# Token-order expert units in groups of four: one 128-row pass each, and four quarter-array passes side by side

## Chip, cores and metric

The kernel runs on 1 core of one Trainium2 chip. The metric is device time in microseconds (us): 950.32 us is the median of 3 runs of the kernel before (950.28 to 957.16). Engines are named as in the profile: PE is TensorE (PEld its weight loads), DVE is VectorE, ACT is ScalarE, POOL is GpSimd, SP is SyncE, which here only issues DMAs.

## What is computed

Four batches of 10048 tokens go through agent attention and then through a two-level mixture of experts. Cut to what matters:

```python
# B, N, C = 4, 10048, 128; 49 agents; 4 groups x 4 experts; F = 1024
a2k = softmax(scale * agents @ k.T)      # 49 x N per batch
agent_v = a2k @ v                        # 49 x 128
q2a = softmax(scale * q @ agents.T)      # N x 49
x = q2a @ agent_v                        # N x 128, rank 49
g = argmax(x @ w_group); e = argmax(x @ w_expert[g])    # one expert of 16 per token
h = relu(x @ w1[g, e])                   # 1024 wide
out = p(g) * p(e) * (h @ w2[g, e])       # p: softmax weights of the choices
```

## The kernel before

**Small rank.** A token's `x` has rank 49, so the kernel never forms it. It keeps the 49 exponentials of `q2a` per token (the tile `ef`), and multiplies `agent_v` (scaled, in the tile `at`) into an expert's `w1` once. An expert's first product is then a product over 49 rows, its second one over the 1024 columns.

**Two halves of a number.** All these products run in fp16 with each operand split into a high part and a low part (the rounded value and what is left of it). A tile `et` holds 512 tokens as columns; its rows 0 to 48 are the high parts, its rows 49 to 97 the low parts of the exponentials. A tile `wbuf` holds an expert's factors: 1024 columns of high parts, 1024 of low parts (both repeated for the two row blocks), then the two halves of `w2`.

**Units.** A unit is 128 of the 1024 columns for a tile of 512 tokens. It has a first product into a PSUM bank `ph`; an eviction (ACT: relu to fp16, tile `hh`; DVE: what is left of it, tile `hl`; `evicted`, line 1197); and a second product, 12 passes of 128 columns into the bank `po` (`second`). A tile of 512 tokens has 8 units and ends with `oo`, a DVE multiplication of `po` by the tokens' weights, and the DMA of the result (`out_rows`).

**Stages.** (1) A front of some 77 us for the first batch (batch 1): keys, values, agents, the first queries. (2) The token-order stage: the batches 1, 2, 3 in turn, each as 20 tiles of tokens in their own order, all with the expert that most of the batch's tokens choose: 60 tiles, 480 units (the last tile of each batch has 384 tokens). (3) The sorted stage: the tokens of batch 0, which were brought into the order of their experts by indirect DMAs, in 19 tiles of 512 and 3 of 256.

**First product, token order.** `first` (line 1204) makes two passes of 98 rows by 512 columns into one of three banks `ph`: the high factors, then the low ones. Up to 8 units lie between a first product and its second (`LAG`).

**First product, sorted.** `first_group` (line 1178) takes four units at once. Each has one pass of 128 rows: 98 rows as above with the high factors, and in the rows 98 to 127 the low factors of the first 30 agents against a copy of the high exponentials. The remaining 19 agents' low factors are four passes of 19 rows, which sit in the four quarters (32 rows each) of the array, one unit per quarter, and write four different banks. For these, a tile `rest` holds four copies of 19 rows of `et`, made by four DMAs on SP's queue (`turn`, line 1176). The banks are three of `ph` and those of the pool `at` in turn.

**Side work.** Beside the units of one batch, the next batches are prepared: scores of keys and queries (`at<-agh,xh` and its like), softmax over agents, routing, the turning of exponentials into `et` (`turned`), all as Python generators. `advance` (line 1375) is called once per unit; it lets lanes of `QUEUE` step while two budgets last (`RATE`: DVE and ACT nanoseconds per unit), the lane that is furthest behind its share (`QUEUE`, `TOTALS`) first. A generator that yields a number is left alone for so many units (`HOP` is 2), so that what it waits for is done by then. The tile framework then orders each engine's instructions; each engine runs its own list in order and waits on semaphores.

**Banks.** PSUM has eight banks: three for `ph`, two for `po`, three for `at` (the side work, and in the sorted stage half of the units).

## Time and profile before

| what | value |
|---|---|
| median of 3 runs | 950.32 us |
| the profiled execution's own time | 955.84 us |
| its span, first to last instruction | 954.1 us |
| mean granted TensorE clock | 0.970 |
| first `ph` of an expert unit, first `rest` pass | 76.8 us, 768.5 us |
| PE, DVE, ACT, POOL busy | 92%, 78%, 65%, 45% of the span |

How to read it: the two marks in the fifth row bound the stages. From 76.8 to 768.5 us lie the 480 token-order units with all side work, from there to 942.5 us (the last `po`) the sorted units with almost none, and some 12 us of closing follow. Busy time is a union of instructions; a PE matmul is shown from its start to its modelled end, some 160 ns after the next one has started, so a pass is timed from its start to the start of the next.

### The profile page before, as it was taken

To read this page: it belongs to the slowest core of one execution; us is meant where nothing else is said; L and a number is where in the kernel's file an instruction comes from. 1 tells how busy PE (TensorE), PEld (TensorE's weight loads), DVE (VectorE), ACT (ScalarE), POOL (GpSimd) and SP (SyncE) were. 2 spreads that over 40 slices of the span, in tenths; PEclk is the share of its full clock that TensorE was granted. 3 is DMA by queue.
4 is the path that set the end of the run, shared out by engine and by line. 5 is a ranking of instruction groups with operands and counts; after the bars stand their busy time and mean duration, and the time that the engine had idled before them with its cause. 6 is when DMAs were issued, how large, how long until landed. Compare 5 with 4: busy or idle time off the path is not lost.

```text
span 954.1 us, 31174 instructions
## 1 busy us (share of the span) xinstructions
PE 875.2 (92%) x12947; PEld 699.0 (73%) x12948; DVE 740.6 (78%) x1619; ACT 619.5 (65%) x1071; POOL 431.6 (45%) x573
## 2 busy tenths in 40 slices
PE   3868998999998989999999999999999999999985
PEld 2765876877776777777778777787777887777864
DVE  5646699889689797769988988989987666667753
ACT  4546777866877767668778677776556555555541
POOL 3164535533743235454355432465555414444434
PEclk9777999999999999999999999999999999999998
DMA  9637534535426444444435231222646445555560
GB/s 314 193 122 241 177 123 120 173 100 161 134 72 196 136 126 134 147 133 130 116 93 155 80 102 49 93 90 90 203 153 202 140 149 197 200 194 203 196 215 29
DMA packets 110461, 140.26 MB, mean 147 GB/s; under 512 B 8374, under 2 KB 90369, under 8 KB 107495
## 3 DMA queue, kind: packets, MB, share of 16 engines
q1 hardware_dynamic: 105159, 127.88, 42.3%
q0 software_dynamic: 5152, 10.30, 3.3%
q8 instruction: 103, 1.69, 0.7%
q14 instruction: 47, 0.39, 0.1%
HBM read 96.83 MB, written 39.99 MB: 143 GB/s over the span
## 4 chain that ended last, share of the span: by engine, by line
PE 54%; DVE 24%; issue 8%; ACT 5%; POOL 5%; DMA 3%; SPq 1%; POOLq 0%; ACTq 0%; DVEq 0%
PE po L135 28%; PE ph L135 15%; PE at L135 11%; DVE hl L135 8%; POOL xl L272 3%; DVE vl L135 3%; DVE S L135 2%; ACT hh L135 2%; DVE oh L135 1%; DMA out<-oo,er 1%; DVE oo L135 1%; DVE rx L135 1%; DVE mq L135 1%; POOL xs L272 1%; DVE ef L135 1%
## 5 line engine op out<-in xcount | busy, mean ns | idle before, releaser
L135 PEld LDWEIGHTS <-hh 128*128 128x128 f16 x5104 | 410.6, 98 | 122.4 <-issue 12.7
L135 PE MATMUL po<-wbuf,hh 128*128 128x128 f16 x5104 | 489.7, 220 | 0.9 <-ACT hh L135 0.8
L135 DVE SCALAR_TENSOR_TENSOR hl<-ph,hh 128x512 f16<-128x512 f32 (+1 forms) x562 | 377.2, 677 | 140.2 <-ACT hh L135 138.1
L135 PE MATMUL po<-wbuf,hl 128*128 128x128 f16 x2552 | 457.7, 220 | 0.0
L135 ACT ACTIVATE hh<-ph 128x512 f16<-128x512 f32 (+1 forms) x562 | 328.4, 592 | 190.3 <-PE ph L135 106.3
L135 PE MATMUL ph<-et,wbuf 98*128 98x512 f16 (+3 forms) x1048 | 319.1, 380 | 23.9 <-DVE hl L135 19.8
L272 POOL TENSOR_TENSOR xl<-xf,xh 128x256 f16<-128x256 f32 x280 | 187.8, 705 | 165.6 <-ACT xh L135 144.0
L135 PEld LDWEIGHTS <-hl 128*128 128x128 f16 x2552 | 249.4, 98 | 0.3 <-issue 0.3
L135 PEld LDWEIGHTS <-wbuf 98*128 98x128 f16 (+2 forms) x1412 | 99.5, 99 | 73.2 <-issue 45.3
L1253 POOL DMA_INDIRECT out<-oo,er x82 | 80.5, 981 | 111.9 <-ACT hh L135 60.7
L998 POOL DMA_INDIRECT sorted_rows<-rows,slot x79 | 78.5, 994 | 68.2 <-ACT hh L135 48.9
L135 ACT ACTIVATE xh<-xf 128x1280 f16<-128x1280 f32 (+2 forms) x59 | 73.5, 1251 | 26.3 <-PE at L135 9.7
L713 POOL TENSOR_TENSOR rows<-ef,rows 128x245 f16<-128x245 f32 (+1 forms) x62 | 41.1, 684 | 74.7 <-ACT rows L135 74.7
L479 POOL TENSOR_TENSOR sl<-S,sh 128x245 f16<-128x245 f32 (+2 forms) x51 | 35.1, 711 | 82.1 <-ACT sh L135 75.9
L135 PEld LDWEIGHTS <-xh 128*128 128x128 f16 (+1 forms) x1164 | 55.1, 99 | 3.8 <-issue 2.3
L135 PE MATMUL at<-agh,xl 128*128 128x49 f16 x523 | 52.2, 185 | 5.6 <-POOL xl L272 5.5
L135 DVE SCALAR_TENSOR_TENSOR hl<-at,hh 128x512 f16<-128x512 f32 x82 | 55.8, 681 | 0.0
L135 PEld LDWEIGHTS <-xl 128*128 128x128 f16 (+1 forms) x582 | 48.5, 98 | 7.5 <-POOL xl L272 7.0
L135 ACT ACTIVATE et<-at 98x512 f16<-98x512 f16 (+1 forms) x80 | 47.3, 593 | 10.4 <-PE at L135 9.9
L135 PE MATMUL at<-agh,xh 128*128 128x49 f16 x523 | 51.9, 186 | 0.6 <-ACT xh L135 0.6
L135 PE MATMUL at<-agl,xh 128*128 128x49 f16 x523 | 51.5, 185 | 0.0
L135 DVE SCALAR_TENSOR_TENSOR vl<-vf,vh 128x640 f16<-128x640 f32 (+2 forms) x51 | 44.8, 890 | 8.5 <-ACT vh L135 6.7
(268 smaller groups left out, 1053.4 us busy)
## 6 DMA issues: line engine op xcount, KB each, us to landing
wbuf<-wdr SPq DMA_DIRECT2D x22, 1024.0 KB
vf<-v SPq DMA_DIRECT2D x28, 640.0 KB
xf<-qT SPq DMA_DIRECT2D x28, 640.0 KB
xf<-kT SPq DMA_DIRECT2D x23, 640.0 KB
out<-oo SPq DMA_DIRECT2D x57, 256.0 KB
erow<-rows SPq DMA_DIRECT2D x12, 490.0 KB
er<-sorted_rows SPq DMA_DIRECT2D x19, 256.0 KB
wbuf<-kT SPq DMA_DIRECT2D x5, 640.0 KB
```

Of the source, the lines that this page charges most:

```text
L135: return f(*a, **k)
L272: pool.tensor_sub(out=xl[:, a:z], in0=xf[:, a:z], in1=xh[:, a:z])
L479: pool.tensor_sub(out=sl[0:m, y][:, z], in0=x[:, z], in1=sh[0:m, y][:, z])
L713: pool.tensor_sub(out=x0[:, a:z, NA:2 * NA], in0=ef[:, a:z], in1=x0[:, a:z, 0:NA])
L998: ins = pool.indirect_dma_start(out=sorted_rows[:, :], out_offset=bass.IndirectOffsetOnAxis(ap=at, axis=0), in_=x, in_offset=None, bounds_ ...
L1253: ins = pool.indirect_dma_start(out=out, out_offset=bass.IndirectOffsetOnAxis(ap=to, axis=0), in_=y, in_offset=None, bounds_check=B * N - ...
```

## The change

It does this:

- `first` goes. Token-order tiles use `first_group` too, for four units at a time: four passes of 128 rows, then the four quarter passes of 19 rows. The units of a group are no longer neighbours: group g has units g, g+2, g+4, g+6 of the 8, so that a quarter of the array always meets the same quarter of the columns; the low factors are stored once (`W2 = F + F // 4` columns ahead of `w2` where there were `2 * F`). The product of two low parts is left out, as in the sorted stage. The very first tile keeps two 98-row passes per unit (`"low" in x`).
- Rows 98 to 127 of `et` are now filled for all batches: `query_split` copies 30 high exponentials more per token (ACT), the transposes turn 128 columns.
- Every token-order tile gets its four `rest` DMAs, a tile ahead (`rest_ahead`).
- `expert_split` makes the mixed factors with one DVE operation more per half (`scalar_tensor_tensor` with the constant `head`), and four SBUF-to-SBUF DMAs for a token-order expert.
- PSUM: four banks for `ph`, one for `po` (two before), three for `at`.
- Pending second products: 4 to 8 units as the groups go, `LAG` is gone. Within a tile's first group side work follows each unit's second product; in its second group the four second products run first, then four `advance` calls in one place.
- The budgets become 700 and 900 with twice that as the most saved up; `HOP` now stands for 2 to 4 units, up to a fixed place in the next group; yields that need not wait so long are 1 or 2.

Cut to its core:

```diff
-RWS = [P // 2 + 2 if b == SORTED else NA for b in range(B)]
+RWS = [P // 2 + (2 if b == SORTED else 0) for b in range(B)]
-RATE = np.array([900.0, 1100.0])
+RATE = np.array([700.0, 900.0])
-HOP = 2
+HOP = 9
-OPENING = (3, 14)
-LAG = 8
+OPENING = (3, 8, 6)
+W2 = F + F // GROUP
+WB = (W2 + 2 * F) // 2
...
-    ps1 = ctx.enter_context(tc.tile_pool(name="ps1", bufs=3, space=PSUM))
-    ps2 = ctx.enter_context(tc.tile_pool(name="ps2", bufs=2, space=PSUM))
+    ps1 = ctx.enter_context(tc.tile_pool(name="ps1", bufs=4, space=PSUM))
+    ps2 = ctx.enter_context(tc.tile_pool(name="ps2", bufs=1, space=PSUM))
...
+    def later(y):
+        return clock[0] + ((4, 3, 2, 2)[clock[0] % GROUP] if y == HOP else y)
...
-        if b == SORTED:
-            act.activation(x0[:, :, 2 * NA:P], ef[:, :, 0:DUP], AF.Copy)
+        act.activation(x0[:, :, 2 * NA:P], ef[:, :, 0:DUP], AF.Copy)
...
+            act.activation(high[:, s], ps, AF.Copy)
+            vec.tensor_sub(out=low[:, s], in0=ps, in1=high[:, s])
             yield
+            vec.scalar_tensor_tensor(out=ws[:, s], in0=high[:, s], scalar=cc("head"), in1=ps, op0=ALU.mult, op1=ALU.add)
+            yield
+        if not whole:
+            for i in range(GROUP):
+                sync.dma_start(out=ws[i * STRIP:(i + 1) * STRIP, F:W2], in_=low[DUP:DUP + STRIP, i * F // GROUP:(i + 1) * F // GROUP])
...
+    def rest_of(et, w):
+
+        rest = ep.tile([P, TS], F16, name="rest", bufs=RSB)
         for j in range(GROUP):
             sync.dma_start(out=rest[j * STRIP:j * STRIP + REST, 0:w], in_=et[DUP:NA, 0:w])
+        return rest
...
+        ks = [i * n // GROUP + g for i in range(GROUP)]
+        units = [psa.tile([P, 512], F32, name="at", tag="at") if "own" not in x and i % 2 else ps1.tile([P, TS], F32, name="ph") for i in range(GROUP)]
+        for k, ps in zip(ks, units):
             for j in range(per):
                 f = (k * per + j) * P
+                o = ps[:, j * m:(j + 1) * m]
+                if "low" in x:
+                    pe.matmul(o, x["wb"][0:2 * NA, f:f + P], x["et"][0:2 * NA, 0:m], start=(j == 0), stop=False)
+                    pe.matmul(o, x["low"][0:2 * NA, f:f + P], x["et"][0:2 * NA, 0:m], start=False, stop=(j == per - 1))
+                else:
+                    pe.matmul(o, x["wb"][:, f:f + P], x["et"][:, 0:m], start=(j == 0), stop=False)
+        for j in range(per if "low" not in x else 0):
+            for i, (k, ps) in enumerate(zip(ks, units)):
+                f = F + (k * per + j) * P - i * F // GROUP
                 s = slice(i * STRIP, i * STRIP + REST)
                 pe.matmul(ps[:, j * m:(j + 1) * m], x["wb"][s, f:f + P], x["rest"][s, 0:m], start=False, stop=(j == per - 1))
+        return [(x, k, *evicted(ps, per * m)) for k, ps in zip(ks, units)]
...
-        np.minimum(tokens + RATE, RATE, out=tokens)
+        np.minimum(tokens + RATE, 2 * RATE, out=tokens)
...
+    def rest_ahead(pos, i):
+        pos, i = (pos, i + 1) if i + 1 < OT else (pos + 1, 0)
+        if pos < NOWN and i in state[SEQ[pos]].get("et", {}):
+            rests[pos, i] = rest_of(state[SEQ[pos]]["et"][i], min(TQ, NT - i * TQ) * P)
...
-        for k in range(units):
-            pending.append(first(x, k))
-            for _ in range(2):
-                if len(pending) > LAG:
-                    run_second()
+        def beside(k):
             advance(at + (k + 1) * each)
             ahead()
+
+        for g in range(units // GROUP):
+            finish = run_second if pos < NOWN else sorted_second
+            while len(pending) > GROUP:
+                finish()
+            done = first_group(x, g)
+            for k, y in enumerate(done):
+                pending.append(y)
+                if len(pending) > GROUP:
+                    finish()
+                if pos < NOWN:
+                    if g == 0:
+                        beside(k)
+                        if k == 1:
+                            rest_ahead(pos, i)
+                    continue
...
+            for k in range(GROUP if pos < NOWN and g else 0):
+                beside(GROUP + k)
```

How it moves instructions, at three places in the middle of the second token-order batch (line 135 of the kernel before is line 138 of the changed one: the helper that records every operation).

PE before, a unit between two second products; the names are the bank, the turned exponentials, the factors:

```order
L135 MATMUL po_7809<-wbuf1_120,hl_7675 128x128
L135 LDWEIGHTS wbuf1_120
L135 MATMUL ph_8013<-et_5787,wbuf1_120 128x512
L135 LDWEIGHTS wbuf1_120
L135 MATMUL ph_8013<-et_5787,wbuf1_120 128x512
L135 LDWEIGHTS hh_7700
L135 MATMUL po_7809<-wbuf1_120,hh_7700 128x128
```

PE in the changed kernel, the end of a group's first products:

```order
L138 MATMUL ph_8138<-et_5808,wbuf1_120 128x512
L138 LDWEIGHTS wbuf1_120
L138 MATMUL ph_8139<-et_5808,wbuf1_120 128x512
L138 LDWEIGHTS wbuf1_120
L138 MATMUL ph_8136<-rest_7770,wbuf1_120 128x512
L138 LDWEIGHTS wbuf1_120
L138 MATMUL ph_8137<-rest_7770,wbuf1_120 128x512
L138 LDWEIGHTS wbuf1_120
L138 MATMUL ph_8138<-rest_7770,wbuf1_120 128x512
L138 LDWEIGHTS wbuf1_120
L138 MATMUL ph_8139<-rest_7770,wbuf1_120 128x512
L138 LDWEIGHTS hh_7982
```

Eight 512-column passes for four units have become four, and four quarter passes right behind them; all four banks are complete only after the last row shown.

DVE before, around the end of a tile (`oo`); `most` is a running maximum of key scores, the `oh` and `rx` rows are routing:

```order
L135 SCALAR_TENSOR_TENSOR hl_8068<-ph_8064,hh_8067 128x512
L135 TENSOR_TENSOR most_7693<-at_7975,most_7693 128x490
L135 SCALAR_TENSOR_TENSOR hl_8108<-ph_8104,hh_8107 128x512
L135 TENSOR_TENSOR oo_8123<-po_7809,cw_6482 128x512
L135 SCALAR_TENSOR_TENSOR hl_8131<-ph_8127,hh_8130 128x512
L135 TENSOR_TENSOR oh_8216<-oh_8216 128x320
L135 TENSOR_TENSOR rx_8319<-lg_7893,oh_8216 128x320
```

DVE in the changed kernel, the same place:

```order
L138 SCALAR_TENSOR_TENSOR hl_7983<-ph_7970,hh_7982 128x512
L138 SCALAR_TENSOR_TENSOR hl_7987<-ph_7971,hh_7986 128x512
L138 SCALAR_TENSOR_TENSOR hl_7991<-ph_7972,hh_7990 128x512
L138 SCALAR_TENSOR_TENSOR hl_7995<-ph_7973,hh_7994 128x512
L138 TENSOR_TENSOR most_7397<-at_7951,most_7397 128x490
L138 TENSOR_TENSOR oo_8098<-po_7854,cw_6760 128x512
L138 TENSOR_REDUCE mq_8134<-at_8070 128x9
L138 TENSOR_TENSOR ef_8256<-at_8070,mq_8134 128x441
L138 SCALAR_TENSOR_TENSOR hl_8149<-ph_8136,hh_8148 128x512
```

`hl` comes in blocks of four, and `oo` stands behind such a block and behind side work. On PE the next tile's first second product (`po_8164`) now needs the one bank that this `oo` reads; it comes after the group `ph_8136` to `ph_8139`.

SP before, then SP in the changed kernel, around the same place:

```order
L242 DMA xf_8341<-qT 128x1280
L1242 DMA out<-oo_8123 128x4x128
L841 DMA ohd2_129<-oh_8216 128x320
L242 DMA xf_8450<-kT 128x1088
L242 DMA xf_9011<-qT 128x1280
```

```order
L245 DMA xf_8676<-qT 128x1280
L1256 DMA out<-oo_8098 128x4x128
L1195 DMA rest_8628<-et_6557 19x512 x4
L245 DMA xf_9159<-qT 128x1280
L725 DMA erow2_124<-rows_7947 128x1280
```

Four `rest` DMAs per tile stand between a tile's result and the loads of the next chunks.

## Prediction

> **What bounds the kernel now.** I read the share of each engine first, then the two stages, then single passes on the time line.

> ```profile
> PE 875.2 (92%) x12947; PEld 699.0 (73%) x12948; DVE 740.6 (78%) x1619; ACT 619.5 (65%) x1071; POOL 431.6 (45%) x573
> ```

> The busy times by stretch, with PE, PEld, DVE, ACT, POOL in this order: the token-order stage, the sorted stage, and 100 us of the former:

> ```profile
> 76.80:768.50 691.70, 657.92 (x9929) 524.32 (x9927) 581.40 (x1280) 490.35 (x835) 322.86 (x446) 0.99 0.43 131
> 768.50:943.00 174.50, 170.36 (x2427) 134.57 (x2426) 114.70 (x187) 93.83 (x184) 76.01 (x78) 0.99 0.54 185
> 550.00:650.00 100.00, 96.05 (x1486) 77.44 (x1486) 88.13 (x222) 71.72 (x133) 43.50 (x59) 1.00 0.23 77
> ```

> The change acts on the first row: 691.7 us, 73% of the span of 954.1. PE is busy for 95% of it, DVE for 84%. So PE sets the pace, and DVE is not far below. In the third row DVE reached 88%, the most of any 100 us that I looked at.

> A unit on PE, token order, from starts to starts:

> ```profile
> 683.01 0.59 PE L135 MATMUL ph<-et,wbuf 98*128 98x512 f16 x2
> 683.44 0.28 PE L135 MATMUL po<-wbuf,hh 128*128 128x128 f16 x2
> ...
> 684.11 0.55 PE L135 MATMUL at<-rh,et 98*128 98x21 f16 x16
> 684.52 0.59 PE L135 MATMUL ph<-et,wbuf 98*128 98x512 f16 x2
> ```

> The two 98-row passes take 0.43 us (683.01 to 683.44), 0.215 each, the second product 0.67 (to 684.11), 16 small side passes 0.41, or 26 ns each. What PE waits for in front of a first product is small in the whole kernel, and DVE's waits are mostly for ACT:

> ```profile
> L135 PE MATMUL ph<-et,wbuf 98*128 98x512 f16 x912 | 275.9, 384 | 19.3 <-DVE hl L135 19.0
> L135 DVE SCALAR_TENSOR_TENSOR hl<-ph,hh 128x512 f16<-128x512 f32 x538 | 364.2, 683 | 137.0 <-ACT hh L135 135.1 <-issue 1.0
> ```

> **The change part by part.** *The first products.* The sorted stage already runs the new form; one group of four on PE:

> ```profile
> 803.81 0.38 PE L135 MATMUL ph<-et,wbuf 128*128 128x512 f16 x1
> 804.02 0.38 PE L135 MATMUL at<-et,wbuf 128*128 128x512 f16 x1
> 804.24 0.38 PE L135 MATMUL ph<-et,wbuf 128*128 128x512 f16 x1
> 804.45 0.38 PE L135 MATMUL at<-et,wbuf 128*128 128x512 f16 x1
> 804.76 0.39 PE L135 MATMUL ph<-rest,wbuf 19*128 19x512 f16 x1
> 804.77 0.38 PE L135 MATMUL at<-rest,wbuf 19*128 19x512 f16 x1
> 804.77 0.39 PE L135 MATMUL ph<-rest,wbuf 19*128 19x512 f16 x1
> 804.77 0.39 PE L135 MATMUL at<-rest,wbuf 19*128 19x512 f16 x1
> 805.09 0.29 PE L135 MATMUL po<-wbuf,hh 128*128 128x128 f16 x2
> ...
> 807.78 0.38 PE L135 MATMUL ph<-et,wbuf 128*128 128x512 f16 x1
> ```

> A pass of 128 rows steps by the same 0.215 us as one of 98. The last of the four steps by 0.31, so 0.095 is lost on the way into the quarters; the four quarter passes start within 0.01 us of each other and end with the way out after 0.33 (804.76 to 805.09). A group's first products take 1.28 us (803.81 to 805.09) where eight passes of 0.215 take 1.72: 0.44 us saved. 480 units less the first tile's 8 are 118 groups; 6 of them belong to the batches' last tiles of 384 columns and save about 0.3. The sum is 112 x 0.44 + 6 x 0.3 = 51 us of PE time.

> [...]

> *The one bank for `po`, and evictions in blocks of four.* Before, a tile's first second product found the other bank free. Now it waits until `oo` has read the only one, and everything behind it on PE waits too: all four second products and the side passes, so in the end DVE and ACT. DVE in the sorted stage, over the same group:

> ```profile
> 801.62 0.69 DVE L135 SCALAR_TENSOR_TENSOR hl<-ph,hh 128x512 f16<-128x512 f32 x1 [1.49 <-ACT hh L135]
> 802.22 0.68 DVE L135 SCALAR_TENSOR_TENSOR hl<-at,hh 128x512 f16<-128x512 f32 x1
> 802.82 0.68 DVE L135 SCALAR_TENSOR_TENSOR hl<-ph,hh 128x512 f16<-128x512 f32 x1
> 803.42 0.68 DVE L135 SCALAR_TENSOR_TENSOR hl<-at,hh 128x512 f16<-128x512 f32 x1
> 804.02 0.68 DVE L135 TENSOR_TENSOR oo<-po,er 128x512 f32<-128x512 f32 x1
> 805.82 0.69 DVE L135 SCALAR_TENSOR_TENSOR hl<-ph,hh 128x512 f16<-128x512 f32 x1 [1.12 <-ACT hh L135]
> ```

> DVE steps by 0.60 for each, and `oo` ends at 804.70, 0.39 us before the second product that will need its bank (805.09); the last `hl` ends at 804.10, 0.35 before the fourth pass of the next group (804.45). That is the spare time without side work. Side work in the token-order stage:

> ```profile
> 77.00:768.00 691.00, 341.99 (x1884) 183.99 (x1884) 320.90 (x480) 0.99 0.43 132
> 77.00:768.00 691.00, 39.79 (x59) 0.00 (x0) 0.99 0.43 132
> 77.00:768.00 691.00, 160.87 (x3313) 8.01 (x56) 69.79 (x138) 79.26 (x132) 0.99 0.43 132
> L135 DVE TENSOR_TENSOR wbuf<-at,wbuf 128x512 f16<-128x512 f32 x9 | 6.2, 688 | 4.9 <-ACT wbuf L135 4.9
> ```

> The rows are those of the tiles `hl` (PE, PEld, DVE), `oo` (DVE, POOL) and `at` (PE, PEld, DVE, ACT). DVE's side work is 581.4 - 320.9 - 39.8 = 221 us; `expert_split` adds one operation of 0.69 to each of the 10 halves made in this stage, 7 us: 228, or 0.47 per unit. PE's side passes take between 3313 x 0.026 = 86 and the 161 of the row, which counts tails; I take 110, 0.23 per unit. Between a group's quarters and `oo` lie three side calls on DVE (1.42 us) and four on PE (0.92): the spare 0.39 shrinks by 0.50 to -0.11. On the mean a tile waits 0.1 us; a tile with more DVE work waits longer, and one with less gives nothing back. I take 0.25 us for each of 60 tiles: +15 us. The bounds: 0, if the spread is small; and the 1.27 us of one conversion on ACT (row below), if each tile's `oo` stands behind a DVE operation that waits for it: +76.

> ```profile
> L135 ACT ACTIVATE xh<-xf 128x1280 f16<-128x1280 f32 x51 | 64.6, 1269 | 20.8 <-PE at L135 8.0 <-DMA xf<-qT 4.0 <-DMA xf<-kT 2.5
> ```

> *Four banks for `ph`.* The 19.3 us of PE's waits for `hl` before a first product may vanish, or become waits for the last bank of a block, whose spare is the 0.35 above. I take 0, with -19 as the bound.

> *The `rest` DMAs.* 59 tiles times 4 issues on SP:

> ```profile
> L1176 SPq DMA_DIRECT2D rest<-et x88: 561/562/779, 763.2 to 924.1; - x88
> SPq L1242 <- DVE oo L135: 168.2, 42, 10.1
> L135 ACT ACTIVATE rows<-ef 128x300 f16<-128x300 f32 x7 | 3.3, 465 | 0.0
> ```

> 236 x 0.56 = 133 us of SP's queue in some 650, beside waits such as the 168 us for `oo`, the longest 10.1. They are queued a tile ahead (10 us and more), so an ordinary wait is covered; the quarter passes would have to wait for the rest of it if SP stood still for longer. What stands behind them, the chunk loads, runs ahead too. I take 0; if one wait of 10.1 us in each batch were uncovered, +30. The 24 copies that ACT gains, 0.465 each, are 11 us on an engine busy for 490 of 692: 0.

> *Opening and sorted stage.* The first expert's factors pass through one DVE operation more per half before the first unit: 2 x 0.69 = +1.4 us (0 to 3, as one half may overlap). The 14 side calls ahead of the first tile become 8 and 6. The sorted stage keeps its form; its single `po` has the 0.39 to spare: 0 (up to 22 tiles x 0.3 = +7).

> The sum: -51 + 15 + 0 + 0 + 1 = -35 us on the profiled execution, whose span is 954.1 and whose time is 955.84. The front, the sorted stage and what lies around the span stay, so I take the same 35 off the median: 950.3 - 35 = **915 us**.

> **The rivals.** *PE alone counts.* DVE's spare is enough, and the four banks end the waits for `hl`: -51 - 19 + 1 = -69, 881 us. For it: PE's 95% against DVE's 84%. Against: DVE's blocks of four come late, as all four banks fill at once.

> *VectorE becomes the floor.* DVE needs 588 us in the stage. If it cannot be used beyond the 88.1% of its best stretch, the stage lasts 588 / 0.881 = 667, 24 less than now: 926 us. For it: the 84% of now, and in-order waits between three engines. Against: DVE's 137 us of waits for `hh`, which side work can fill in the new order. [...]

> *The single bank costs more than the passes save (slower).* The wait for `oo` at the end of each tile decides from (51 - 1) / 60 = 0.83 us a tile on. At its bound of 1.27 us it costs 76: -51 + 76 + 1 = +26, 976 us. For it: `oo` now stands behind four `hl` and behind side operations that wait for ACT. Against: some 2 us of PE work lie between the last second product of a tile and the first of the next, the group's 1.28 among them.

> *The quarters do not run side by side* with four banks of one pool: then a group has eight passes and the two switches, 0.2 us more than before, 118 x 0.2 = +24, 974 us. Against it stand the four starts within 0.01 us above.

> **How the numbers follow.** Forecast 0.45; PE alone 0.17; DVE's floor 0.25; the single bank 0.10; quarters in turn 0.03. The time is the forecast's 915. Its own range is 900 to 928. The range that holds 8 in 10 takes in DVE's floor with a few us of the DMAs' bound, and the upper half of what lies toward PE alone: 888 to 940. About 1%, 9.5 us, is what a measurement of this kernel can tell from no change. Faster by more: the forecast, PE alone and most of DVE's floor, 0.82. Within 1%: the rest of that and a bank that costs about what the passes save, 0.07. Slower: 0.11.

> **What would show it.** In the changed profile the stage from the first unit to the first sorted tile should last some 655 us with 480 units; a group's first products should step by 1.28 us and its quarters start together (else the last rival). PE's idle time before `po` that ends with DVE `oo` should be about 15 us over 60 tiles; over 50 would make the forecast wrong on the slow side, near 0 on the fast side. DVE's share of the stage should be about 90%; if PE's idle time ends with `hl` or ACT instead, DVE's floor was right. PE waiting for a `rest` DMA would show that SP's cover failed. The sorted stage should keep its 174 us.

## The result and the profile after

| | before | changed |
|---|---|---|
| median of the runs (lowest to highest), us | 951.88 (950.28 to 957.16) | 964.76 (960.57 to 969.18) |
| profiled execution: time / span, us | 955.84 / 954.1 | 965.79 / 963.9 |
| first `oo` to the 60th (token-order stage), us | 674.7 | 687.6 |
| 60th `oo` to the last (sorted stage), us | 170.8 | 167.9 |

The changed kernel is slower by 1.3%: ratio 1.0126, 95% interval 1.0098 to 1.0153. Forecast were 915 us and a range of 888 to 940. The whole loss is in the token-order stage (+12.9), which takes 703 us from its first unit to the first sorted tile (78.4 to 781.3), not the forecast 655; its first `oo` comes at the same time (97.1 for 97.3), and the sorted stage is 2.9 shorter.

First the passes themselves. Two groups of the changed kernel on PE's time line, in a stretch without side work; the columns are the start, the length of the row, the operation and how many instructions the row holds:

```profile
753.15 1.03 PE L138 MATMUL ph<-et,wbuf 128*128 128x512 f16 x4
754.11 0.40 PE L138 MATMUL ph<-rest,wbuf 19*128 19x512 f16 x4
754.43 0.28 PE L138 MATMUL po<-wbuf,hh 128*128 128x128 f16 x2
...
757.12 1.03 PE L138 MATMUL ph<-et,wbuf 128*128 128x512 f16 x4
```

From 753.15 to 754.43 are the forecast 1.28 us, and the four quarters together take 0.40 us where one takes 0.38: they run side by side. Of the 1.28 us, 0.10 go on the way into the quarters (753.15 to 754.11, less four steps of 0.215) and by an estimate as much on the way out (754.11 to 754.43, less one such step). Where no side work is left, a tile steps by 8.0 us instead of 8.8 (twice 3.97, as 753.15 to 757.12). So the 0.44 us a group is there, and it comes off the end where PE has nothing else to wait for.

Now the stretch with side work. I cut both kernels at the first and the 41st `oo`: 40 tile steps, 80 groups. The row holds the length, then the busy time of PE, PEld, DVE, ACT and POOL (with counts), the granted clock and the DMAs' share and rate; before, then changed:

```profile
97.31:583.37 486.06, 458.56 (x7290) 370.91 (x7289) 408.45 (x834) 361.93 (x609) 219.03 (x327) 0.99 0.43 128
```
```profile
97.12:598.03 500.91, 451.64 (x7311) 355.70 (x7307) 415.74 (x855) 365.49 (x637) 219.57 (x337) 0.96 0.45 136
```

The changed kernel needs 14.9 us more here, with PE busy for 7 us less and idle for 49.3 us instead of 27.5, and at a lower clock. In the rest of the stage (41st to 60th `oo`) it needs 1.9 less: 186.7 for 188.6. What PE waited for (total, times, longest): in the 40 steps before, in the 40 steps of the changed kernel, and in its whole stage:

```profile
PE ph L135 <- DVE hl L135: 16.4, 16, 2.6
```
```profile
PE ph L138 <- DVE hl L138: 13.9, 32, 1.7
PE po L138 <- DVE oo L138: 12.3, 11, 3.1
```
```profile
PE po L138 <- DVE oo L138: 21.5, 19, 3.1
PE ph L138 <- DVE hl L138: 16.3, 43, 1.7
```

Before it was 16.4 us for `hl` and nothing for `oo`. So a new wait for `oo` has come, and the old one for `hl` stayed. The new one is not spread over the 60 tiles: the 21.5 us are 19 waits of 1.1 us on the mean. The clock is the second loss. The longest wait for `oo`, in cells of the clock record (3.41 us each: the shortest stretch in the record, and in both traces every other stretch but the last is a whole number of these; columns as above):

```profile
356.50:359.90 3.40, 3.27 (x44) 2.38 (x41) 3.40 (x7) 2.84 (x5) 1.07 (x2) 1.00 0.30 85
359.90:363.30 3.40, 0.39 (x7) 0.39 (x7) 3.40 (x8) 1.96 (x4) 2.88 (x4) 1.00 0.08 24
363.30:366.70 3.40, 3.40 (x35) 3.40 (x33) 3.39 (x10) 0.00 (x0) 0.00 (x0) 0.50 0.81 212
366.70:370.10 3.40, 3.40 (x55) 2.26 (x53) 2.40 (x11) 1.61 (x3) 0.00 (x0) 1.00 0.84 242
```

In the second cell PE works for 0.39 us; the third runs at half clock, and PE gets 35 instructions done in it where 55 fit into the fourth. The steps of second products show it directly, within the third cell and behind it:

```profile
365.43 0.42 PE L138 MATMUL po<-wbuf,hh 128*128 128x128 f16 x2
365.65 0.31 PE L138 MATMUL po<-wbuf,hl 128*128 128x128 f16 x1
365.75 0.42 PE L138 MATMUL po<-wbuf,hh 128*128 128x128 f16 x2
...
366.88 0.28 PE L138 MATMUL po<-wbuf,hh 128*128 128x128 f16 x2
366.99 0.22 PE L138 MATMUL po<-wbuf,hl 128*128 128x128 f16 x1
367.04 0.28 PE L138 MATMUL po<-wbuf,hh 128*128 128x128 f16 x2
```

Three products step by 0.32 us (365.43 to 365.75) at half clock and by 0.16 (366.88 to 367.04) at full. So this pause of 3.13 us was paid for by another 1.7, an estimate: half of a cell. In the whole stage 10.2 us were at half clock before, 47.8 now; by steps against those of the same kind at full clock, PE lost some 4.7 us to it before and 20.7 now. VectorE in front of this `oo`:

```profile
355.61 2.42 DVE L138 SCALAR_TENSOR_TENSOR hl<-ph,hh 128x512 f16<-128x512 f32 x4
357.94 0.25 DVE L138 TENSOR_TENSOR oh<-oh,rc 128x200 f16<-128x200 f16 x1
358.11 0.82 DVE L138 SCALAR_TENSOR_TENSOR vl<-vf,vh 128x640 f16<-128x640 f32 x1
...
361.55 0.70 DVE L138 TENSOR_TENSOR rd<-lg,gm 128x80 f32<-128x80 f32 x1
362.17 0.68 DVE L138 TENSOR_TENSOR oo<-po,cw 128x512 f32<-128x512 f32 x1
```

Between the block of four `hl` and `oo` stand 4.2 us of side operations (357.94 to 362.17). PE's next second product needs the single `po` bank and starts at 362.91, just behind `oo`.

### The profile page after: what moved, and what is told of

It is laid out like the page before. It is cut to its first block, busy times and chain, and to the rows that moved or that the text cites. A ratio compares the mean times of both kernels' runs of the same rounds, so it can differ in the third digit from the quotient of the medians.

```text
span 963.9 us, 31598 instructions
## 1 busy us (share of the span) xinstructions
PE 853.7 (89%) x12947; PEld 670.5 (70%) x12948; DVE 746.7 (77%) x1631; ACT 611.5 (63%) x1095; POOL 424.1 (44%) x573
## 4 chain that ended last, share of the span: by engine, by line
PE 30%; DVE 14%; ACT 3%; issue 2%; POOL 1%; DMA 1%; SPq 0%; POOLq 0%; ACTq 0%; DVEq 0%
PE po L138 19%; PE ph L138 6%; DVE hl L138 6%; PE at L138 5%; ACT hh L138 1%; POOL out L1267 1%; DVE oo L138 1%; DVE vl L138 1%; DVE oh L138 1%; DVE rd L138 1%; DVE mq L138 1%; ACT lg L138 1%; DMA wbuf<-wdr 1%; DVE rx L138 0%; DVE wbuf L138 0%
## 5 line engine op out<-in xcount | busy, mean ns | idle before, releaser
L138 PE MATMUL po<-wbuf,hh 128*128 128x128 f16 x5104 | 474.3, 223 | 25.6 <-DVE oo L138 22.5
L138 DVE SCALAR_TENSOR_TENSOR hl<-ph,hh 128x512 f16<-128x512 f32 (+1 forms) x562 | 352.0, 675 | 110.0 <-ACT hh L138 108.6
L138 ACT ACTIVATE hh<-ph 128x512 f16<-128x512 f32 (+1 forms) x562 | 295.5, 597 | 166.6 <-PE ph L138 92.0
L138 PE MATMUL ph<-et,wbuf 128*128 128x512 f16 (+3 forms) x568 | 168.8, 381 | 17.8 <-DVE hl L138 16.3
L138 PEld LDWEIGHTS <-wbuf 128*128 128x128 f16 (+1 forms) x1404 | 81.2, 96 | 147.1 <-issue 98.9
L138 PE MATMUL ph<-rest,wbuf 19*128 19x512 f16 (+2 forms) x560 | 72.8, 384 | 2.3 <-DMA wbuf<-low 2.3
L138 PE MATMUL at<-agh,xl 128*128 128x49 f16 (+1 forms) x532 | 52.7, 186 | 7.0 <-POOL xl L275 7.0
L138 PE MATMUL at<-agh,xh 128*128 128x49 f16 (+1 forms) x532 | 52.9, 186 | 4.4 <-ACT xh L138 1.6
L138 PEld LDWEIGHTS <-xl 128*128 128x128 f16 x582 | 48.3, 98 | 9.9 <-POOL xl L275 9.9
L138 PE MATMUL at<-agl,xh 128*128 128x49 f16 (+1 forms) x532 | 52.5, 185 | 0.0
```

The lines of the kernel that those rows point to most:

```text
L138: return f(*a, **k)
```

## The experiments

My theory after reading the two traces: `oo` and `hl` come late because VectorE works through its line in order (above, `oo` behind 4.2 us of side operations), PE pauses at their banks, and the half clock that follows doubles the loss. The rivals: the one bank for `po` itself; VectorE's load as such; groups broken up in PE's order; the planner's new constants; the side calls in one place; array switches (the ways into the quarters and out) that cost more than the 0.10 us or so each that they show above.

Ratios are to runs of before beside the same runs, with 95% intervals. In eight of the runs (chips 3 and 8 on record) before took 952 us. In the ten others (chips 0, 4 and 9: spread, spread_again, oo_first_next_place, side_ahead, dose, dose_po, the two with two full passes, and the two with `oo` early and other rates) before itself took 965 to 967 us, and the new orders paused from about 620 us on with no releaser in the trace: PE for 9.6 us of the stage in the run called dose, never in the changed kernel's own profile. That run, which is the changed kernel up to the sorted stage, took 716.8 us for the stage. So whole times of the ten are compared only among themselves, and with the others over the first 40 tile steps, which lie ahead of these pauses: the changed kernel's own order took 500.9 us there in its own profile, 497.9 (dose) and 501.5 (dose_po) among the ten. Each length is that of one profiled execution, and with these three 3.6 us apart a difference of less than some 4 us says little.

### Is it the single bank? Is it VectorE's load?

Two banks for `po` again, and the last unit of a group in one of the side work's three banks:

```diff
-    ps1 = ... bufs=4 ...   ps2 = ... bufs=1 ...
+    ps1 = ... bufs=3 ...   ps2 = ... bufs=2 ...
-        units = [psa.tile(...) if "own" not in x and i % 2 else ps1.tile(...) for i in range(GROUP)]
+        units = [psa.tile(...) if (i == 3 if "own" in x else i % 2) else ps1.tile(...) for i in range(GROUP)]
```

> The changed kernel (964.8 us) with two banks for the second product again and three for the first ones; the fourth unit of a token-order group takes a bank of the pool of the side work. Theory A, the single bank: PE's 21.5 us of waits for the end-of-tile multiplication (DVE) in the token-order stage fall below 5, and with them a part of the 48 us at half clock; the time falls by 22 to 35 us, to 930 to 943. Theory B, VectorE is the floor (it is busy for 85 to 93% of the stage): the waits reappear before the first products or before side passes, and the time stays within 8 us of 965. Theory C, the blocks of four and the side work in one place cost it: as B.

Measured: 966.45 us, 1.0144 (1.0107 to 1.0182), as the theories B and C had it. The wait for `oo` is gone, but PE now waits for `hl` at the bank that was taken from the side work; the first 40 steps, 506.0 us long:

```profile
PE at L138 <- DVE hl L138: 14.4, 16, 2.3
PE ph L138 <- DVE hl L138: 6.9, 14, 1.9
```

`oo` first in VectorE's line: the side calls of a tile's first group also go behind its four second products.

```diff
-                    if g == 0:
-                        beside(k)
-                        if k == 1:
-                            rest_ahead(pos, i)
+                    if g == 0 and k == 1:
+                        rest_ahead(pos, i)
                     continue
...
-            for k in range(GROUP if pos < NOWN and g else 0):
-                beside(GROUP + k)
+            for k in range(GROUP if pos < NOWN else 0):
+                beside(g * GROUP + k)
```

> The changed kernel with the side work of a tile's first group also in one place, behind the four second products, so that on DVE the end-of-tile multiplication stands right behind the block of four evictions, with no side operation between; the single bank stays. Theory A (what costs is that this multiplication stands behind side work while PE has one bank): its waits fall from 21.5 to below 8 us, the half clock falls from 48 us, the time to 935 to 948. Theory B, VectorE is the floor: 957 to 970. Theory C, side work in one place costs by itself: over 965, since now both groups have it.

Measured: 950.46 us, 0.9984 (0.9961 to 1.0008): 14 us below the changed kernel, level with before. The first 40 steps, and their waits:

```profile
98.84:587.85 489.01, 452.66 (x7322) 353.62 (x7318) 410.36 (x854) 364.33 (x633) 220.58 (x335) 0.97 0.45 139
```
```profile
PE ph L138 <- DVE hl L138: 13.6, 32, 2.6
...
PE po L138 <- DVE oo L138: 2.8, 3, 1.7
```

PE's idle time falls from 49.3 to 36.4 us, and the stage's waits for `oo` from 21.5 to 4.7. So with one `po` bank it counts what stands ahead of `oo` on VectorE: 11.9 us of these 40 steps. Whether two banks would do as well if none had to be taken from the side work is not shown, since no kernel here uses more than eight in all, and each uses eight. The wait for `hl` stays.

Half of VectorE's `hl` work left out (the low parts of columns 256 to 511 of every token-order unit; second products read the other half instead):

```diff
...
-        vec.scalar_tensor_tensor(out=hl[:, 0:m], in0=ps[:, 0:m], scalar=0.0, in1=hh[:, 0:m], op0=ALU.max, op1=ALU.subtract)
+        z = min(m, z)
+        vec.scalar_tensor_tensor(out=hl[:, 0:z], in0=ps[:, 0:z], scalar=0.0, in1=hh[:, 0:z], op0=ALU.max, op1=ALU.subtract)
...
+                if "own" in x:
+                    s = slice(q % 2 * P, (q % 2 + 1) * P)
                 pe.matmul(o, hl[:, s], wt[:, 0:C], start=False, stop=(c == n - 1 and j == per - 1 and q == w - 1))
```

> The changed kernel with half the low parts of the token-order evictions: DVE computes 256 of 512 columns, and the second products use these twice, so that half of the low parts are wrong ones while PE's work is the same. DVE loses some 472 times 0.27 us, 127 us. Theory B, VectorE is the floor: PE's waits for DVE nearly vanish (43 us in all of the token-order stage to below 10), the half clock too (48 us to below 15), and the time falls to 900 to 920, where the forecast without DVE's part lay. Theory A alone: the end-of-tile multiplication still waits for side operations, so 935 to 950.

Measured: 955.05 us, 1.0048 (1.0019 to 1.0078): slower than either forecast. The first 40 steps:

```profile
98.40:592.90 494.50, 444.33 (x7302) 355.17 (x7301) 348.07 (x855) 364.42 (x637) 221.29 (x338) 0.96 0.45 138
```
```profile
PE po L138 <- DVE oo L138: 13.9, 10, 3.6
PE ph L138 <- DVE hl L138: 6.0, 6, 2.2
```

VectorE has 68 us less to do (348.1 for 415.7) and the stretch gets 6.4 shorter; the wait for `oo` is as long as ever. VectorE's total is not the floor. With both edits together:

> Leaves out half of the low parts hl of the token-order units (columns 256 to 511), as the run with half of them did, but with oo right behind the hl of its block. Theory A (oo and hl stand in VectorE's line behind operations that wait for ACT; both waits must go): with oo early and hl half as long, waits for oo near 5 us and for hl near 6 us, PE idle under 35 us in the stage, half clock under 30 us: 938 us. Theory D (other waits, for at, xl and the like, take the place of those removed): 948 to 952 us, PE idle still above 42 us.

Measured: 948.0 us, 0.9923 (0.989 to 0.9956); the first 40 steps 484.7 us, PE idle for 44 us in the stage (10.8 of it still for `oo`) and 50 us at half clock. The rival came nearer (PE's idle time stayed above 42 us). What a sixth less load on VectorE adds to `oo` early is small: 2.5 us by the medians, some 6 by the ratios to before, 4.3 in the first 40 steps.

### Is it the order inside the groups, or the planner?

In the changed kernel's trace 19 of the 118 groups are broken: another pass of PE, a side pass or a second product, stands between a group's first pass and its last quarter, in 11 of them between the quarters. The later passes and the quarters kept in their written order:

```diff
-                    pe.matmul(o, x["wb"][:, f:f + P], x["et"][:, 0:m], start=(j == 0), stop=False)
+                    y = pe.matmul(o, x["wb"][:, f:f + P], x["et"][:, 0:m], start=(j == 0), stop=False)
+                    if "own" in x and k != ks[0]:
+                        tc.keep_in_program_order(y)
...
-                pe.matmul(ps[:, j * m:(j + 1) * m], x["wb"][s, f:f + P], x["rest"][s, 0:m], start=False, stop=(j == per - 1))
+                y = pe.matmul(ps[:, j * m:(j + 1) * m], x["wb"][s, f:f + P], x["rest"][s, 0:m], start=False, stop=(j == per - 1))
+                if "own" in x:
+                    tc.keep_in_program_order(y)
```

> The changed kernel with one thing added: inside a group of four of the token-order stage, the three later 128-row passes and the four quarters keep their written order, so that no side pass comes between them (182 runs of quarters become 166 for 162 groups). Theory B (broken groups take back part of the saving; about 20 more switches of array mode at some 0.42 us, 8 us): 956 us, PE time in the stage about 8 us less, waits as in the changed kernel (po for oo about 21 us, half clock about 48 us). Theory A (PE's pauses at the single po bank and at hl, and the half clock behind them, are the loss; broken groups only use up time that PE would wait anyway): 963 to 968 us, the saved PE time comes back as waits for hl or oo.

> The same order inside a group, together with all side work of a tile's first group behind its four second products, so that oo follows right behind the hl of its block. If the two add up: 950.5 less 8 = 943 us, with waits of po for oo under 6 us. If the order only shifts time into waits (theory A): 949 to 953 us, the waits for hl growing from 18 us.

Measured: 965.71 us, 1.016 (1.0127 to 1.0193), and with `oo` early 952.49, 0.9998 (0.9982 to 1.0013): nothing gained in either. The first 40 steps of the former:

```profile
99.00:597.20 498.20, 440.91 (x7303) 349.77 (x7301) 416.41 (x856) 364.43 (x637) 219.81 (x338) 0.97 0.45 137
```
```profile
PE po L138 <- DVE oo L138: 15.4, 13, 3.4
PE ph L138 <- DVE hl L138: 14.6, 40, 1.5
```

The quarters are broken in 4 groups now, but a first pass still stands apart, so that 20 groups are not whole. PE is busy for 10.7 us less than in the changed kernel, the stretch is 2.7 shorter: 8 us came back as idle time. So the 8 us that the theory of the broken groups put on PE did go, and were worth nothing in time. With `oo` early the stage's waits for `hl` grew from 18.4 to 23.6 us, as the other theory had it.

The planner's constants put back:

```diff
-RATE = np.array([700.0, 900.0])
+RATE = np.array([900.0, 1100.0])
-        return clock[0] + ((4, 3, 2, 2)[clock[0] % GROUP] if y == HOP else y)
+        return clock[0] + (2 if y == HOP else y)
-        np.minimum(tokens + RATE, 2 * RATE, out=tokens)
+        np.minimum(tokens + RATE, RATE, out=tokens)
```

> The changed kernel with the constants of the side-work planner put back (rates 900 and 1100 for 700 and 900, the store of tokens capped at one rate and not two, the short distance of 2 calls at each place). Theory C (the planner's new constants bunch the side work of VectorE and so cause the waits): 950 us or less, waits of po for oo under 12 us and half clock under 30 us. Theory A (waits come from where the side calls stand, not from their rates): 960 to 970 us, with oo waits of 15 us or more.

Measured: 974.72 us, 1.023 (1.0201 to 1.026), 20.4 us of waits for `oo` in the stage and 61 us at half clock. Slower than either forecast: the first 40 steps took 492.6 us, but with 7 us less work of VectorE in them (408.4 for 415.7), and side work was left for the end (from the 41st to the 60th `oo` 200.0 us for 186.7). PE also waited for `rest` here, 5.2 us in six waits. The new constants do not cause the loss: the whole time without them is longer. The old rates and the old cap with `oo` early, and higher rates with `oo` early:

> The version with oo right behind the hl of its block, with the planner's old rates of 900 and 1100 and its old cap of one rate (distances as changed). With the changed order the old rates and distances made the first 40 tiles 8 us shorter (492.6 for 500.9) but the whole 10 us longer, as side work was left for the last tiles. If the cap alone spreads side work better: 940 to 946 us where the version itself takes 0.998 of before. If side work is left over again: 955 to 965 us. On a chip where before takes 965 us all this is 1.5 to 5% longer.

> As the run with oo right behind the hl of its block, with the planner's rates at 850 and 1100 instead of 700 and 900. If side work that comes earlier and in even portions is what is missing: 942 to 947 us. If rates do not matter (the waits come from the place in line): 948 to 953 us.

Among the ten: 997.1 us, 1.0333 (1.0281 to 1.0384), and 999.91, 1.0345 (1.0297 to 1.0394); first 40 steps 487.4 and 490.8 us for 489.0: no difference that these steps can tell.

### Where side work stands

The one place undone: the last group's side calls one behind each second product, as in the first group.

```diff
                 if pos < NOWN:
-                    if g == 0:
-                        beside(k)
-                        if k == 1:
-                            rest_ahead(pos, i)
+                    beside(g * GROUP + k)
+                    if g == 0 and k == 1:
+                        rest_ahead(pos, i)
                     continue
...
-            for k in range(GROUP if pos < NOWN and g else 0):
-                beside(GROUP + k)
```

> The changed kernel with one part undone: the side calls of a tile's last group stand one behind each of its second products, as those of its first group do, and no longer in one place. Theory A (what counts is how near in front of oo and of hl side operations stand that wait for ACT; the first group, where oo is, keeps its calls): little changes, 960 to 970 us, waits of po for oo still near 20 us. Theory E (the calls that are put into one place leave no time between the steps of a side chain, and the engines stall in line there): about 950 us, with fewer waits for hl and half clock under 35 us.

> The kernel of the run called spread, on another chip if it so falls. By the stretch of that run that was not disturbed (oo of the 10th to oo of the 42nd tile: 410.3 us, against 402.4 for the changed kernel's own order on the same chip) the one place is worth about 8 us: 970 to 976 us. Theory E (the one place costs): 950 us.

Measured: 1011.58 us, 1.0496 (1.0427 to 1.0565), and again 1015.94, 1.0494 (1.0459 to 1.0529); first 40 steps 503.4 and 504.1 us, against 497.9 to 501.5 for the changed kernel. The one place is worth some 4 us here at most, half of what I had read from the stretch between the 10th and the 42nd `oo` before; it costs nothing.

Two variants of the version with `oo` early. In one, every step of a side chain that had a distance of one or two calls waits for the next group (`y in (1, 2, HOP)` in `later`); in the other, the last group's four side calls stand ahead of its second products:

> As the run with oo right behind the hl of its block, and every step of a side chain that named a distance of one or two calls now waits for the next group, so that no chain has two dependent steps in one place. Theory E (dependent steps in one place stall VectorE and ACT in line and so make hl late): waits for hl fall from 18 to under 10 us and the time from 950.5 to about 938 us. Theory A (VectorE's in-order place is enough): 946 to 956 us, as chains that are spread further only shift work to later tiles.

> As the run with oo right behind the hl of its block, but the four side calls of a tile's last group stand ahead of its second products instead of behind them, so that TensorE does its side passes while hl is still being written, and VectorE's side operations behind this block find their inputs ready. Theory A: waits for hl fall from 18 to about 10 us in the stage and the time from 950.5 to 940 to 945 us. Rival: the side passes themselves wait there for ACT and GpSimd, since the calls now stand only a group's first products behind those of the group before: 950 to 960 us, with waits for at above 15 us.

Measured: 1090.05 us, 1.129 (1.1244 to 1.1337), and 1009.24, 1.0412 (1.0348 to 1.0476). Both fell short. In the first, side work was left over and was done at once before the sorted stage, two steps of 59 and 60 us; its first 40 steps took 497.4 us, 8 more than with `oo` early alone, though less side work was done in them. In the second they took 500.5; the wait for `hl` in them did not fall (13.6 us, as with `oo` early alone).

### What the quarters are worth in this order

The quarter passes left out (the low parts of the first products of token order, save in the first tile):

```diff
...
-        for j in range(per if "low" not in x else 0):
+        for j in range(per if "own" not in x else 0):
```

> The changed kernel without the quarter passes of the token-order tiles (but for the first tile), so the low factors of 19 agents are left out of their first products; all else, the DMAs for the quarters too, stays. PE loses 117 times some 0.42 us, 49 us. If PE's own work still sets the pace: 916 to 925. Theory B, VectorE or the waits between the engines set it: 945 to 965, with PE's idle time up by 30 us or more. Theory A allows some 940, as the four banks of a group still end together and the multiplication still comes late.

Measured: 928.46 us, 0.9753 (0.9706 to 0.98), between the forecasts and nearer to the one in which PE's work sets the pace; PE's idle time in the stage grew by 12 us (75.2 for 63.3), not by 30. And the reverse: a second 128-row pass over the high parts in place of each quarter (the low parts are left out, save in the first tile), so that a group has the eight passes of before in the new order, and no way into quarters and out:

```diff
             for i, (k, ps) in enumerate(zip(ks, units)):
+                if "own" in x:
+                    f = (k * per + j) * P
+                    pe.matmul(ps[:, j * m:(j + 1) * m], x["wb"][:, f:f + P], x["et"][:, 0:m], start=False, stop=(j == per - 1))
+                    continue
                 f = F + (k * per + j) * P - i * F // GROUP
```

> Leaves out the low parts of the first products of the token-order stage (but for the first tile) and runs the 128-row pass over the high parts a second time in their place: the new order with its one po bank, its four ph banks and its side calls in one place, but with the eight full-width passes of before in each group and no switch of array mode. If the arrangement is what costs and the quarters keep their worth of 0.44 us in each of 112 groups: 965 + 49 = 1014 us. If TensorE's pauses take most of it, as the pauses at oo and hl shrink when TensorE has more of its own to do: 975 to 990 us, with the waits for oo and hl together falling from 38 to under 20 us in the stage and half clock from 48 to under 25 us. Rival: the switches cost more than they show, 955 to 965 us.

> Leaves out the low parts of the first products of the token-order stage (but for the first tile) and repeats the 128-row pass over the high parts in their place, in the version with oo right behind the hl of its block. Compared over the first 40 token-order tiles, which took 489.0 us with quarters in that version. Theory A (VectorE's late oo took the quarters' worth back, and with oo early they are worth something again): 505 us or more, so that the quarters are worth 16 us or more of the 35. Rival (any saving of TensorE's is taken back here, by hl if not by oo): 489 to 496 us.

Measured: 1016.19 us, 1.0505 (1.0459 to 1.0551), where the changed kernel with its one place undone took 1015.94 beside it; with `oo` early 1005.59, 1.0415 (1.0362 to 1.0468). The first 40 steps: without quarters, with two passes (and their waits), with two passes and `oo` early:

```profile
99.20:566.90 467.70, 411.59 (x6996) 350.71 (x6995) 413.09 (x842) 358.24 (x632) 224.23 (x335) 0.95 0.47 145
```
```profile
98.54:601.70 503.16, 465.17 (x7302) 371.34 (x7301) 417.06 (x854) 364.41 (x637) 219.16 (x337) 0.99 0.45 136
```
```profile
PE ph L138 <- DVE hl L138: 10.4, 29, 1.3
PE po L138 <- DVE oo L138: 8.2, 5, 2.6
```
```profile
97.19:588.19 491.00, 462.59 (x7299) 368.99 (x7298) 412.15 (x854) 363.62 (x633) 219.76 (x335) 0.99 0.45 140
```

This is the test that settles most. By steps on PE (start to next start, less the idle time before the next; the first four columns add up to the length within 1.3 us):

| first 40 tile steps, us | `ph` passes and quarters | second products | side passes | gaps between PE instructions | at half clock | length |
|---|---|---|---|---|---|---|
| before | 139.4 | 219.1 | 99.9 | 27.5 | 10.2 | 486.1 |
| changed | 120.5 | 226.1 | 104.7 | 48.3 | 44.4 | 500.9 |
| two full passes | 146.2 | 217.1 | 101.3 | 37.6 | 13.7 | 503.2 |
| no quarters | 77.4 | 224.2 | 109.4 | 55.7 | 44.4 | 467.7 |
| `oo` early | 122.3 | 223.9 | 106.1 | 36.3 | 34.1 | 489.0 |
| `oo` early, two full passes | 145.8 | 215.3 | 101.1 | 28.3 | 6.8 | 491.0 |

With two full passes PE has 25.7 us more of first products than the changed kernel, and the stretch is 2.3 us longer. With `oo` early it is 23.5 us more for 2.0. So of the 35 us that 80 groups should save the quarters are worth some 2, no more than these 40 steps can tell. Of the 25.7, 10.7 went into idle time and 12.4 into slower second products and side passes, nearly all of that in steps at half clock (44.4 us of it for 13.7). And the arrangement alone, with the passes of before, costs 17 us against before (503.2 for 486.1), 12 of which `oo` early gives back (491.0).

Against a simple "PE does not matter here" stands the run without quarters: 43 us less of first products made the stretch 33 shorter. From no quarters to two full passes it is 35.5 us of length for 68.8 of passes, about half. Why the quarters sit at nearly the full length of two passes and not between is not settled; what the runs show is that the half clock is as frequent as without any (44.4 each), and falls to 13.7 with two full passes. This also speaks against array switches that cost more than they show: the run without quarters has no such passes in these steps, and yet the same half clock and more gaps.

### Do pauses lead to the half clock?

Idle operations of VectorE ahead of some `oo` of the sorted stage; in the first run on constants, in the second, whose edit is shown, as extra writes of `oo` itself from the `po` bank:

```diff
+        n0 = dict.fromkeys(range(5, 9), 2) | dict.fromkeys(range(9, 13), 4) | dict.fromkeys(range(13, 17), 6)
+        for _ in range(n0.get(len(dose), 0)):
+            vec.tensor_mul(out=o[:, 0:n], in0=po[:, 0:n], in1=x["c"][:, 0:n].broadcast_to([P, n, C]))
```

> The changed kernel with idle operations of VectorE of some 0.6 us put ahead of oo in part of the sorted stage, where no other wait disturbs: 2 in each of four tiles, then 4 in each of four, then 6 in each of four. Theory A (a TensorE pause of more than about half of a 3.41 us cell of the clock record is followed by a cell at half clock): with 2 (pause near 0.8 us) the step of a tile grows by the pause alone, from 8.2 to 9.0 us, and the clock stays full; with 4 (pause near 2 us) and 6 (near 3.2 us) cells at half clock follow the pauses and the step grows by some 1 to 1.7 us more than the pause, to 11 to 12 us and 12.5 to 13.5 us. Rival (the half clock belongs to other causes of the token-order stage, not to pauses): steps of 9.0, 10.2 and 11.4 us, the clock full throughout. The time is 956 to 1010 us with either.

> The changed kernel with oo written several times in part of the sorted stage, each time read from the po bank, so that the bank is held longer: 2 extra operations of 0.60 us in each of four tiles, then 4 in each of four, then 6 in each of four. Steps of 8.18 us without. By the spare of 0.39 us the pauses are 0.8, 2.0 and 3.2 us. Theory A (a cell of 3.41 us of the clock record with TensorE busy for less than about half of it is followed by one at half clock): steps of 9.0 us at full clock with 2; 10.2 us plus 1 to 1.7 with 4 and 11.4 us plus 1 to 1.7 with 6, each such tile with a cell at half clock. Rival (pauses by themselves do not lead to the half clock): 9.0, 10.2 and 11.4 us, full clock throughout.

Measured: the first was no dose at all, since its operations did not need the bank and ran in VectorE's waits (steps of 8.2 to 9.8 us, pauses up to 1.2 us, full clock; 1009.45 us, 1.045, 1.0365 to 1.0534). In the second (1059.99 us, one run) the steps were 9.6 to 10.2 us with 2 extra, full clock; 12.2 to 12.5 with 4, and one cell at half clock in four tiles; 13.6 to 14.5 with 6, with cells at half clock in each of the four tiles. So the half clock came with the longer doses; but with 4 extra a step grew by 4 us where a pause of 2.0 was forecast (`hl` came late too), nearly without half clock, so that the price of a pause is not shown by it.

The count over all 20 profiled kernels is clearer. Every cell of 3.41 us at full clock of the token-order stage, by the share in which PE was busy, and how many were followed by one at half clock:

| PE busy in the cell | below 0.4 | 0.4 to 0.5 | 0.5 to 0.6 | 0.6 to 0.7 | 0.7 to 0.8 | 0.8 to 0.9 | 0.9 and more |
|---|---|---|---|---|---|---|---|
| cells | 90 | 53 | 106 | 177 | 301 | 425 | 2665 |
| followed by half clock | 90 | 42 | 45 | 30 | 15 | 2 | 1 |

Pauses that add up to some 1.7 to 2 us of one cell (PE busy for 0.4 to 0.5 of it) were enough in 42 of 53 cells. By a count from the first to the 60th `oo`, 209 of the 223 cells ahead of a fall to half clock touched no single pause of 3 us.

## Why the prediction was wrong

- *The passes.* Right as an operation: 1.28 us a group, quarters side by side, 0.8 us less per tile without side work. So the rival of quarters in turn is refuted.
- *The step that failed: the sum takes 51 us of PE time off the span one for one* ("The sum: -51 + 15 + 0 + 0 + 1 = -35"), because PE was busy for 95% of the stage. In the first 40 steps that term is 35 us, and the runs with two full passes give 2 for it. Already the passes saved only 18.9 us there (139.4 to 120.5, where 80 groups of 1.28 are 102.4): groups were broken, and some ran at half clock or ended in a pause. Against that stand 20.8 us more of gaps (27.5 to 48.3) and 11.8 more of second products and side passes. So PE's saving came back as waiting and as slower steps. My reading is a ring that sets the length: PE's passes, `hh` on ACT, `hl` and `oo` on VectorE with side operations in line between them, and the banks back to PE. The edits show the part of it where `oo` stands (12 us); the rest of the ring is argued from the waits.
- *No term for the clock.* The profile of before had it (10.2 us at half clock in the stage, PEclk at 0.99), and nothing in the sum asked what more pauses would do to it. PE's loss there went from 4.7 to 20.7 us: +16, about a third of the 50 between 915 and 964.8, if all of it lies on the path.
- *The single bank.* Taken as +15 for the stage; 21.5 us of waits were measured, below the 50 that I had named as the sign of a miss on the slow side. That sign was the wrong one. The 0.25 a tile came from a mean of 1.42 us of side work ahead of `oo`; in the longest wait it was 4.2, and 19 waits made up the sum. The arrangement as a whole cost 17 us in the first 40 steps, where the prediction's 0.25 a tile makes 10.
- *The mechanism given for it* was half right: `oo` does stand behind side operations on VectorE, and `oo` early gains 14 us; but a second bank, taken from the side work, gains nothing. So the rival "single bank costs more than the passes save" has the sign but not the size: its price of 0.83 us a tile was not reached (21.5 / 60 = 0.36), and the slower time came because the passes' saving went too.
- *VectorE as the floor* (926 us): refuted as a matter of load; it is busy for 576 of 687.6 us, 84% where 90 were forecast, and 68 us less of it made 6.4. *PE alone counts*: refuted; the waits for `hl` stayed at 16.3 us for 19.8, as the 0 taken for the four banks had it.
- *`rest` DMAs and opening.* Right at 0: no wait of PE for `rest` among the largest, 2.3 us once for a weight's low part; the first `oo` is 0.2 us earlier.

In the first 40 steps, then: forecast -35 + 10 = -25; measured -2 for the quarters and +17 for the arrangement, +15. Of the versions that leave nothing out none is clearly faster than before; `oo` early is level with it (0.9984).

## What to carry over

A high busy share of an engine, here PE's 95%, does not make its time the time of the stage: ask which ring of engines and banks closes on each tile, and price a saving by what would wait next. On TensorE a pause can cost more than itself: where the pauses made up more than half of a 3.41 us cell, the next was at half clock in 132 of 143 cells here, by an estimate up to 1.7 us more (half of a cell). The most telling test of a saving is to put the old cost back into the new arrangement: here 25.7 us of passes made 2.3 of length.
